# Attention beside a cosine feed-forward: a step's curve, from its sine on, is written behind the next step's attention products

## The chip, the cores and the metric

One core of a Trainium2 chip runs the whole program. The metric is device time of one execution, in microseconds; the profile's span is the time from the first instruction to the last of one profiled execution. TensorE (PE) multiplies, VectorE (DVE), ScalarE (ACT) and GpSimd (POOL) do the elementwise work, and SyncE (SP) issues most DMAs. Each takes its instructions in the order of the program.

## The reference

```python
def _attn_ref(q, k, v):                       # q, k, v: 8 x 8 x 576 x 64
    scores = scale * np.matmul(q, k.transpose(0, 1, 3, 2))
    mask_local = (rel >= 0) & (rel < stride)  # heads 0 to 3; stride 32
    mask_strided = (rel >= 0) & (pos[None, :] % stride == pos[:, None] % stride)  # heads 4 to 7
    scores = np.where(masks[None, :, :, :], scores, -1000000000.0)
    attn = np.exp(scores - np.max(scores, axis=-1, keepdims=True))
    attn = attn / (np.sum(attn, axis=-1, keepdims=True) + 1e-09)
    return np.matmul(attn, v)
...
    x = attn_out.transpose(0, 2, 1, 3).reshape(4608, 512)
    h = x @ w_in                              # 512 x 2048
    g = h * np.cos(h)
    return g @ w_out                          # 2048 x 512
```

## The kernel before

**Tokens and steps.** The 4608 tokens are 12 blocks of 384. A block of the feed-forward takes 16 steps, one for each 128 columns of the hidden layer. Numbers are split into a high and a low part (`g_hi`, `g_lo`), so a product takes three matmuls. The step f of block j, in `hidden`, makes 12 matmuls into one of two PSUM banks, `a` and `b` in turn (line 527), and then the curve h cos h: ScalarE scales h to whole turns (`k`, line 533), VectorE reduces (line 534), ScalarE takes the sine (line 537), VectorE multiplies by h (line 542), which frees the bank, ScalarE casts to `g_hi` (line 547) and GpSimd makes the rest `g_lo` (line 548). `chunk` writes one step: `hidden`, the softmax work of attention units, and `outer` (line 555), 9 matmuls into the accumulators `acc0` to `acc2` for the step three before.

**Attention among the steps.** The attention of batches 0 and 1 and blocks 0 and 1 come first (to 187 us). In blocks 2 to 5 (steps n = 3 to 63, some 188 to 510 us) the attention of the other six batches runs among the steps: 42 units, in each batch strided, strided, local, strided, strided, local, local. The table `bursts` says at which step a unit begins. A **burst** stands ahead of a step's hidden products on TensorE: the products of an earlier unit (line 441 strided, 370 local) and the scores of a new one (lines 405 and 339). There are three banks: scores in `acc0`, transposes and half of the local products in `acc1`, products in `acc2`. Line 431 copies the transposed probabilities out of `acc1`, lines 378 and 379 copy local products out of `acc1` and `acc2`, line 449 strided ones out of `acc2`. The transposes of line 427 follow the step's hidden products.

**Softmax of a unit.** VectorE adds the mask out of the score bank (line 282) and takes maxima (283), GpSimd subtracts them (284), ScalarE takes two silus (293, 296), VectorE joins them (297), ScalarE squares (300), VectorE sums and inverts (302, 305), and GpSimd multiplies (306). A local unit's result is turned by VectorE (351) a good step later; a strided one's is transposed by TensorE (427).

**Other work of a step.** Put behind the step's curve by `behind`: splitting the next block's x (lines 473, 486), sums of weight parts for the later blocks (`combine`: GpSimd 608 and 616, VectorE 613, ScalarE 615), weights on their way out (`put_away`, line 637, on SP's queue), and staging (744, 745). A finished row of attention leaves from ScalarE's queue (line 517).

**What sets the order.** `in_turn` ties TensorE's matmuls together as they are written. On the other engines a scheduler orders the instructions; the order in which they are written is the priority, and `order` adds single ties. One such tie (line 288 and 293) holds a unit's silu behind the copies of the products written last (`self.copied`).

Of the kernel before, what the change touches and what calls it, by code (L numbers as in the profile page):

```python
# [13 lines left out]
F32 = mybir.dt.float32  # L14
# [4 lines left out]
AF = mybir.ActivationFunctionType  # L19
ALU = mybir.AluOpType  # L20
# [33 lines left out]
NFC = DFF // P  # L54

LAG = 3
# [14 lines left out]
LOAD_AT = 6  # L71
# [20 lines left out]
def attention_cos_ffn(ctx, tc, qkl, vl, qkvs, w_in, w_out, eye, eye16, mask_l0, mask_l, mask_s, out):  # L92
# [33 lines left out]
    def order(later, first, reason):  # L126
        tc.add_manual_dep(
            later.ins, first.ins.name,
            mybir.DependencyInfo(mybir.DependencyClass.NoSync, mybir.DependencyReason.DATA), reason=reason,
        )  # L130
# [386 lines left out]
                nc.scalar.dma_start(out=xT[:, c, lo:hi], in_=x[:, lo - at:hi - at])  # L517

    hiddens = itertools.count()

    made_early = {}

    def hidden(j, f, x_hi, x_lo, begun=False):
        h = ps_h.tile([P, 512], F32, name="ab"[next(hiddens) % 2])[:, :TB]
        ops = [(w, x, c) for c in range(NKC) for w, x in ((wi_h, x_hi), (wi_h, x_lo), (wi_l, x_hi))]
        for i, (w, x, c) in enumerate(ops):
            mm = nc.tensor.matmul(h, w[f][:, c], x[c], start=(i == 0), stop=(i == len(ops) - 1))  # L527
            if j >= 2 or begun:
                in_turn(mm)

        r = rp.tile([P, TB], F32, name="r")
        k = r.bitcast(I32)
        nc.scalar.activation(out=k, in_=h, func=AF.Copy, scale=1.0 / (2.0 * math.pi), bias=0.25)
        red = nc.vector.scalar_tensor_tensor(out=r, in0=k, scalar=-2.0 * math.pi, in1=h, op0=ALU.mult, op1=ALU.add)  # L534
        if j < 2:
            reduced[j, f] = red
        sin = nc.scalar.activation(out=r, in_=r, func=AF.Sin, bias=quarter)  # L537
        if j < 2:
            sines[j, f] = sin
        if j == 0 and f == 0:  # L540
            order(sin, exps[-1], "one change of tables")
        chain["curve"] = nc.vector.tensor_tensor(out=r, in0=r, in1=h, op=ALU.mult)  # L542
        if begun:
            g_hi, g_lo = (w[NFC - 1 - f].rearrange("p c n -> p (c n)")[:, :TB] for w in (wi_h, wi_l))
        else:
            g_hi, g_lo = (gp.tile([P, TB], F32R, name=name) for name in ("g_hi", "g_lo"))
        chain["cast"] = nc.scalar.copy(out=g_hi, in_=r)  # L547
        chain["rest"] = nc.gpsimd.tensor_tensor(out=g_lo, in0=r, in1=g_hi.bitcast(F32), op=ALU.subtract)  # L548
        return g_hi, g_lo

    def outer(j, f, g_hi, g_lo, acc, tiles=range(NTT)):
# [25 lines left out]

    pend = []

    def chunk(j, f, x, acc, transposed=(), scored=()):  # L580
        pend.append((j, f, *(made_early.pop((j, f), None) or hidden(j, f, *x)), acc))
        for unit in (*transposed, *scored):
            next(unit)
        if len(pend) > LAG:
            outer(*pend.pop(0))

    def accumulators(pool):
        return [pool.tile([P, DM], F32, name=f"acc{t}") for t in range(NTT)]

    def burst(multiplied, scored):  # L590

        products, tiles = next(multiplied) if multiplied else ((), None)
        scores, others = next(scored) if scored else ((), None)
        if tiles == others:
            matmuls = [m for pair in itertools.zip_longest(products, scores) for m in pair if m]
        else:
            matmuls = [*products, *scores]
        for matmul in matmuls:
            matmul()
        if multiplied:  # L600
            next(multiplied, None)

    def combine(sp, q):

# [156 lines left out]
    with ExitStack() as attending:  # L761
        ps = attending.enter_context(tc.tile_pool(name="ps", bufs=1, space=bass.MemoryType.PSUM, reuse_waits="tile"))
        summing = ExitStack()
        sp = summing.enter_context(tc.tile_pool(name="sp", bufs=1, reuse_waits="tile"))
        att = Attention(attending, False, *(((ps, f"acc{i}"),) for i in range(3)), ld_bufs=2)
        units = [unit for b in range(2, B) for unit in att.units(b)]
        begun = np.interp(range(len(units) + UNIT_LAG), [n for _, n in KNOTS], [at for at, _ in KNOTS])
        bursts = {}
        multiplied = {}
        for kind in (False, True):  # L770
            alike = [k for k in range(len(units)) if bool(STRIDED[k % len(STRIDED)]) == kind]
            multiplied.update(zip(alike[KIND_LAG:], alike))
        left = sorted({*range(len(units))} - {*multiplied.values()})
        multiplied.update(zip(range(len(units), len(units) + UNIT_LAG), left))
        for k, at in enumerate(begun.astype(int).tolist()):
            bursts.setdefault(at, []).append(
                [units[m] if 0 <= m < len(units) else None for m in (k - TURN_LAG, multiplied.get(k, -1), k)]
            )
        putting = put_away()
        sums, last = [], []  # L780
        for q in range(NQ):
            parts = 6 * [combine(sp, q)]
            sums += [last + parts[:1], *([part] for part in parts[1:5])]
            last = parts[5:]
        sums.append(last)
        nxt = direct[3] = x_operands()
        for n in range(LAG, (PLAIN - 2) * NFC):
            j, f = 2 + n // NFC, n % NFC
            if f == 0:
                cur, acc = nxt, accumulators(ps_o)  # L790
            transposed, scored = [], []
            for turned, *units_ in bursts.get(n, ()):
                burst(*units_)
                if turned:
                    transposed.append(turned)
                if units_[1]:
                    scored.append(units_[1])
            if f == LOAD_AT and 2 < j < PLAIN - 1:
                nxt = load_x(j + 1)

            chunk(j, f, cur, acc, transposed, scored)
            if SPLIT_AT <= f < SPLIT_AT + NKC and 2 < j < PLAIN - 1:
                split_loaded(nxt, f - SPLIT_AT)
            next(putting, None)
            if n >= SUMS_AT and sums:
                for part in sums.pop(0):
                    next(part, None)
            if n == STAGED_AT:
                assert not sums
                summing.close()  # L810
                xg = ctx.enter_context(tc.tile_pool(name="xg", bufs=1, reuse_waits="tile"))
                a_pieces = in_pairs(in_xs + in_slots(range(X_AT, X_AT + 6))), in_pairs(
                    in_slots(range(X_AT + 6, X_AT + 20))
                )
                staged = [staging(xg, 0, k, a_pieces[k]) for k in range(2)]
            if n in STAGED:
                next(staged[STAGED[n]])

    rp2, gp2, hp, up, yp = (
        ctx.enter_context(tc.tile_pool(name=name, bufs=bufs, side="right", reuse_waits="tile"))  # L820
# [218 lines left out]
```

## Time and profile before

| | |
|---|---|
| median of 3 runs | 906.04 us (905.9 to 906.94) |
| the profiled execution | 905.24 us, its span 903.2 us |
| TensorE, VectorE, ScalarE, GpSimd busy | 98%, 56%, 58%, 48% of the span |
| granted TensorE clock | 0.998 of full speed |
| HBM read and written | 125.4 MB and 39.6 MB, 183 GB/s over the span |

Engines run side by side, so the shares don't add up. A busy share near 100% says which engine has no time left; what an idle share of another engine is worth has to be read from what it waits for.

### The profile page before, as it was taken

The numbers are of one execution on the slowest core, as the hardware profiler recorded it, in microseconds if no ns is written. First come the engines' busy times: TensorE is split into PE (matmuls) and PEld (weight loads), VectorE is DVE, ScalarE is ACT, GpSimd is POOL, SyncE is SP. The second block draws the span as 40 slices with busy tenths as digits, with TensorE's granted clock in tenths as the row PEclk, the third lists the DMA queues.
The fourth block names the chain that finished last, engine by engine and source line by source line (L and its number), as shares of the span: only waits on it lengthen the run. The fifth ranks groups of instructions, "written<-read, shape, count | busy, mean of one in ns | idle before, by whom it ended". The sixth has DMA issues, their size and how long they took to land.

```text
span 903.2 us, 20455 instructions
## 1 busy us (share of the span) xinstructions
PE 888.3 (98%) x7872; PEld 781.9 (87%) x7872; DVE 501.7 (56%) x966; ACT 522.0 (58%) x1093; POOL 434.8 (48%) x466
## 2 busy tenths in 40 slices
PE   8899999999999999999999999999999999999998
PEld 5689999988888888888888889898998999898997
DVE  5767556455656555556663356555564555554453
ACT  3777777466666656666665455445555545544454
POOL 2766665435756576666744524333343334222231
PEclk9999999999999999999999999999999999999999
DMA  8734334145578867454546756556675656755401
GB/s 292 241 130 142 139 139 161 36 164 175 191 242 278 284 223 239 139 185 139 172 143 217 237 161 221 188 195 209 199 269 173 226 164 197 247 186 187 140 24 70
DMA packets 93408, 166.32 MB, mean 184 GB/s; under 512 B 10752, under 2 KB 34304, under 8 KB 93312
## 3 DMA queue, kind: packets, MB, share of 16 engines
q1 hardware_dynamic: 85248, 157.59, 53.1%
q10 hardware_dynamic: 8064, 7.44, 2.4%
q8 instruction: 62, 1.02, 0.5%
q14 instruction: 34, 0.28, 0.1%
HBM read 125.40 MB, written 39.58 MB: 183 GB/s over the span
## 4 chain that ended last, share of the span: by engine, by line
PE 64%; POOL 4%; ACT 2%; issue 2%; DVE 1%; DMA 0%; SPq 0%; POOLq 0%; ACTq 0%
PE acc L875 22%; PE a L846 11%; PE acc L555 9%; PE b L846 8%; PE b L527 5%; PE a L527 4%; PE acc L370 1%; POOL g_lo L548 1%; POOL t_sb L284 1%; PE acc L441 1%; PE acc L339 1%; PE acc L427 1%; ACT raised L293 1%; DVE r L542 1%; POOL sr L616 0%
## 5 line engine op out<-in xcount | busy, mean ns | idle before, releaser
L861 POOL TENSOR_TENSOR g_lo<-r,g_hi 128x384 fp32r<-128x384 f32 x96 | 98.8, 1030 | 247.7 <-ACT g_hi L860 144.9
L548 POOL TENSOR_TENSOR g_lo<-r,g_hi 128x384 fp32r<-128x384 f32 x94 | 102.4, 1090 | 178.5 <-ACT g_hi L547 101.5
L875 PE MATMUL acc<-s,g_hi 128*128 128x512 f32 x576 | 179.7, 393 | 0.0
L555 PE MATMUL acc<-s,g_hi 128*128 128x512 f32 x564 | 177.6, 396 | 0.0
L555 PEld LDWEIGHTS acc<-s,g_hi 128*128 128x128 f32 x564 | 103.1, 188 | 15.2
L875 PEld LDWEIGHTS acc<-s,g_hi 128*128 128x128 f32 x576 | 106.2, 188 | 10.8
L875 PE MATMUL acc<-s,g_lo 128*128 128x512 f32 x288 | 112.8, 392 | 0.0
L555 PE MATMUL acc<-s,g_lo 128*128 128x512 f32 x282 | 109.8, 390 | 0.0
L527 PE MATMUL a<-x_hi,s 128*128 128x384 f32 x384 | 108.6, 343 | 0.0
L527 PE MATMUL b<-x_hi,s 128*128 128x384 f32 x384 | 108.4, 343 | 0.0
L855 DVE SCALAR_TENSOR_TENSOR r<-r,h 128x384 f32<-128x384 int32 x96 | 58.3, 607 | 88.3 <-ACT r L854 88.3
L846 PE MATMUL a<-s,s 128*128 128x384 f32 x384 | 83.2, 338 | 0.0
L857 DVE TENSOR_TENSOR r<-r,h 128x384 f32<-128x384 f32 x96 | 70.3, 733 | 22.0 <-ACT r L856 20.6
L856 ACT ACTIVATE r<-r,biases 128x384 f32<-128x384 f32 x96 | 59.2, 617 | 36.7 <-DVE r L855 36.6
L860 ACT CAST g_hi<-r 128x384 fp32r<-128x384 f32 x96 | 49.2, 512 | 46.1 <-DVE r L857 45.9
L854 ACT ACTIVATE r<-h 128x384 int32<-128x384 f32 x96 | 50.5, 526 | 40.0 <-DVE h L924 26.0
L846 PEld LDWEIGHTS a<-s,s 128*128 128x128 f32 x384 | 69.4, 188 | 4.2
L537 ACT ACTIVATE r<-r,biases 128x384 f32<-128x384 f32 x96 | 58.6, 611 | 24.5 <-DVE r L534 21.9
L527 PEld LDWEIGHTS b<-x_hi,s 128*128 128x128 f32 x384 | 70.1, 188 | 2.7
L527 PEld LDWEIGHTS a<-x_hi,s 128*128 128x128 f32 x384 | 70.1, 188 | 2.6
L547 ACT CAST g_hi<-r 128x384 fp32r<-128x384 f32 x94 | 48.2, 513 | 35.9 <-DVE r L542 33.5
L527 PE MATMUL a<-x_lo,s 128*128 128x384 f32 x192 | 64.5, 336 | 0.6 <-POOL x_lo L473 0.6
(147 smaller groups left out, 1732.6 us busy)
## 6 DMA issues: line engine op xcount, KB each, us to landing
s<-wis SPq DMA_DIRECT2D x168, 256.0 KB, 3.0
s<-wos SPq DMA_DIRECT2D x96, 256.0 KB, 3.7
qk<-in_qkvs SPq DMA_DIRECT2D x32, 324.0 KB, 3.7
qk<-in_qkl SPq DMA_DIRECT2D x24, 416.0 KB, 4.5
raw<-in_w_in SPq DMA_DIRECT2D x16, 512.0 KB, 4.4
raw<-in_w_out SPq DMA_DIRECT2D x16, 512.0 KB, 3.6
wos<-s SPq DMA_DIRECT2D x32, 256.0 KB, 4.3
wis<-sr SPq DMA_DIRECT2D x32, 256.0 KB, 2.4
```

The lines of the kernel that those rows point to most:

```text
L527: mm = nc.tensor.matmul(h, w[f][:, c], x[c], start=(i == 0), stop=(i == len(ops) - 1))
L537: sin = nc.scalar.activation(out=r, in_=r, func=AF.Sin, bias=quarter)
L548: chain["rest"] = nc.gpsimd.tensor_tensor(out=g_lo, in0=r, in1=g_hi.bitcast(F32), op=ALU.subtract)
L555: mm = nc.tensor.matmul(acc[t], g[:, ts], w[f], start=(f == 0 and i == 0), stop=(f == NFC - 1 and i == 2))
L846: in_turn(nc.tensor.matmul(bank, w[:, n, c], part, start=start and i == 0, stop=stop and i == len(ops) - 1, skip_group_check=True,))
L854: nc.scalar.activation(out=k, in_=h, func=AF.Copy, scale=1.0 / (2.0 * math.pi), bias=0.25)
L855: nc.vector.scalar_tensor_tensor(out=r, in0=k, scalar=-2.0 * math.pi, in1=h, op0=ALU.mult, op1=ALU.add)
L856: nc.scalar.activation(out=r, in_=r, func=AF.Sin, bias=quarter)
L857: chain["curve"] = nc.vector.tensor_tensor(out=r, in0=r, in1=h, op=ALU.mult)
L860: chain["cast"] = nc.scalar.copy(out=g_hi, in_=r)
L861: chain["rest"] = nc.gpsimd.tensor_tensor(out=g_lo, in0=r, in1=g_hi.bitcast(F32), op=ALU.subtract)
L875: in_turn(nc.tensor.matmul(acc, g[gn][:, ts], w[wn], start=done == 0 and i == 0, stop=done == NFC - 1 and i == 2,))
```

## The change

Within blocks 2 to 5, `hidden` no longer writes the second half of its curve (sine, multiplication, cast, rest). It puts these four into `held`, and the loop writes them after the burst of the next step, ahead of that step's own products. The work that stands behind the curve (`work`: splits, weights out, sums; and staging) moves with it. If the burst had local products, the sine is also tied behind the copy of line 379. So a step now writes: burst, the curve of the step before, its work, its own hidden products, k and reduction, softmax, outer products.

```diff
+    held = []
...
-    def hidden(j, f, x_hi, x_lo, begun=False):
+    def hidden(j, f, x_hi, x_lo, begun=False, hold=False):
...
-        sin = nc.scalar.activation(out=r, in_=r, func=AF.Sin, bias=quarter)
...
-        chain["curve"] = nc.vector.tensor_tensor(out=r, in0=r, in1=h, op=ALU.mult)
...
-        chain["cast"] = nc.scalar.copy(out=g_hi, in_=r)
-        chain["rest"] = nc.gpsimd.tensor_tensor(out=g_lo, in0=r, in1=g_hi.bitcast(F32), op=ALU.subtract)
+        def curve(first=None):
+            sin = nc.scalar.activation(out=r, in_=r, func=AF.Sin, bias=quarter)
+            if first is not None:
+                order(sin, first, "copies first")
...
+            chain["curve"] = nc.vector.tensor_tensor(out=r, in0=r, in1=h, op=ALU.mult)
+            chain["cast"] = nc.scalar.copy(out=g_hi, in_=r)
+            chain["rest"] = nc.gpsimd.tensor_tensor(out=g_lo, in0=r, in1=g_hi.bitcast(F32), op=ALU.subtract)
+
+        if hold:
+            held.append(curve)
+        else:
+            curve()
         return g_hi, g_lo
...
         if multiplied:
             next(multiplied, None)
+        return tiles == "32x64"
...
-        for n in range(LAG, (PLAIN - 2) * NFC):
+        def work(n):
             j, f = 2 + n // NFC, n % NFC
-            if f == 0:
-                cur, acc = nxt, accumulators(ps_o)
-            transposed, scored = [], []
-            for turned, *units_ in bursts.get(n, ()):
-                burst(*units_)
...
-            chunk(j, f, cur, acc, transposed, scored)
             if SPLIT_AT <= f < SPLIT_AT + NKC and 2 < j < PLAIN - 1:
                 split_loaded(nxt, f - SPLIT_AT)
             next(putting, None)
             if n >= SUMS_AT and sums:
                 for part in sums.pop(0):
                     next(part, None)
+        def closed():
+            while held:
+                held.pop()(att.copied if local else None)
+
+        for n in range(LAG, steps):
+            j, f = 2 + n // NFC, n % NFC
+            transposed, scored, local = [], [], False
+            for turned, *units_ in bursts.get(n, ()):
+                local = burst(*units_) or local
...
+            closed()
+            if n > LAG:
+                work(n - 1)
...
+            chunk(j, f, cur, acc, transposed, scored, True)
```

TensorE's order is the same in both programs. On ScalarE, at the step whose hidden products begin at 358.38 us (a burst with local products ahead of it), from its k activation to its last cast; before the change (line 537 is the sine, 547 and 615 the casts, 378 and 379 the copies of local products, 293, 296 and 300 the silus and the square):

```order
L533 ACTIVATE r<-b 128x384
L293 ACTIVATE raised_2544<-t_sb,biases 128x6x54
L296 ACTIVATE t_sb<-t_sb,biases 128x324
L537 ACTIVATE r<-r,biases 128x384
L300 ACTIVATE raised_2544<-raised_2544 128x6x54
L547 CAST g_hi<-r 128x384
L615 CAST sr<-sf 128x256
L378 COPY x_l<-acc_5243 128x192
L379 COPY x_l<-acc_5242 128x192
L517 DMA xT<-x_l 128x192 x2
```

and with the change, where the sine is line 544, the casts are lines 552 and 626, and k is line 534:

```order
L534 ACTIVATE r<-b 128x384
L293 ACTIVATE raised_2544<-t_sb,biases 128x6x54
L296 ACTIVATE t_sb<-t_sb,biases 128x324
L300 ACTIVATE raised_2544<-raised_2544 128x6x54
L378 COPY x_l<-acc_5229 128x192
L379 COPY x_l<-acc_5228 128x192
L544 ACTIVATE r<-r,biases 128x384
L517 DMA xT<-x_l 128x192 x2
L552 CAST g_hi<-r 128x384
L626 CAST sr<-sf 128x256
```

The copies moved ahead of the sine, and the square with them; the sine, the DMA issues and both casts follow. Eleven of the 18 local bursts of this part have their sine moved behind softmax work in this way; at the other seven little softmax work stands there, and the copies move ahead of sine and cast alone.

On VectorE, around the multiplication of 271.63 us (line 542; 534 is the reduction, 351 the turn of a local unit, which reads what GpSimd's line 306 writes), before:

```order
L302 TENSOR_REDUCE z<-raised_2543 128x6
L305 RECIPROCAL z<-z 128x6
L534 SCALAR_TENSOR_TENSOR r<-r,b 128x384
L542 TENSOR_TENSOR r<-r,b 128x384
L613 TENSOR_TENSOR sf<-a_3750,sf 128x256
L351 STREAM_TRANSPOSE pt_l<-t_sb 128x384
L282 TENSOR_TENSOR t_sb<-acc_2559,ml 128x384
```

and with the change (multiplication 551, reduction 535):

```order
L302 TENSOR_REDUCE z<-raised_2543 128x6
L305 RECIPROCAL z<-z 128x6
L535 SCALAR_TENSOR_TENSOR r<-r,b 128x384
L351 STREAM_TRANSPOSE pt_l<-t_sb 128x384
L551 TENSOR_TENSOR r<-r,b 128x384
L624 TENSOR_TENSOR sf<-a_3750,sf 128x256
L282 TENSOR_TENSOR t_sb<-acc_2559,ml 128x384
```

The turn moved ahead of the multiplication. The same is so at the copies of 223, 316 and 368 us. On GpSimd, line 306 moved ahead of the rest of the curve at most of the local bursts.

On ScalarE, from the k activation of 419.06 us, before:

```order
L533 ACTIVATE r<-a 128x384
L431 COPY pt<-acc_6231 128x324
L293 ACTIVATE raised_2544<-t_sb,biases 128x6x64
L537 ACTIVATE r<-r,biases 128x384
L296 ACTIVATE t_sb<-t_sb,biases 128x384
L547 CAST g_hi<-r 128x384
L300 ACTIVATE raised_2544<-raised_2544 128x6x64
L449 COPY x_t<-acc_6264 128x6x18x3
```

and with the change:

```order
L534 ACTIVATE r<-a 128x384
L431 COPY pt<-acc_6227 128x324
L544 ACTIVATE r<-r,biases 128x384
L552 CAST g_hi<-r 128x384
L293 ACTIVATE raised_2544<-t_sb,biases 128x6x64
L449 COPY x_t<-acc_6256 128x6x18x3
L296 ACTIVATE t_sb<-t_sb,biases 128x384
L300 ACTIVATE raised_2544<-raised_2544 128x6x64
```

Sine and cast moved ahead of the first silu here. In three other steps (the sines of 320.41, 350.31 and 373.33 us) the sine alone moved ahead of the silus. On SP's queue the weights on their way out (line 637) stand behind the loads that the next burst's units make, by about a step.

## Rows read from the trace of the kernel before

**Rows 1.** The page's head: the span, and each engine's busy us, share of the span and instructions.
```profile
span 903.2 us, 20455 instructions
PE 888.3 (98%) x7872; PEld 781.9 (87%) x7872; DVE 501.7 (56%) x966; ACT 522.0 (58%) x1093; POOL 434.8 (48%) x466
```
**Rows 2.** Busy time by stretch of blocks 2 to 5 (from:to, length, then each engine's busy us and instructions, the granted clock, the share of DMA and its GB/s).
```profile
187.60:350.00 162.40, 162.26 (x2203) 141.46 (x2203) 95.78 (x218) 104.90 (x238) 100.62 (x125) 1.00 0.71 230
350.00:455.00 105.00, 101.76 (x1503) 87.41 (x1504) 63.48 (x141) 66.83 (x156) 66.66 (x82) 1.00 0.51 168
```
**Rows 3.** All waits of TensorE's matmuls from 187.6 to 510 us: who waited for whom, us in total, times, the longest.
```profile
PE acc L427 <- ACT x_l L378: 3.2, 4, 1.1
```
**Rows 4.** TensorE in order of time (start, us, engine, line, tiles, then the idle time before it and what ended it): the start of a step's hidden products (L527) and its transposes (L427), at an undisturbed step and at those that wait; L339 are scores, which follow the local products of L370.
```profile
263.69 0.52 PE L427 MATMUL acc<-ident,pn_s 128*128 128x128 f32 x3
...
271.99 0.45 PE L527 MATMUL a<-x_hi,s 128*128 128x384 f32 x1
...
274.19 0.49 PE L427 MATMUL acc<-ident,pn_s 128*128 128x128 f32 x3
...
357.57 0.87 PE L339 MATMUL acc<-qk 64*32 64x64 f32 x48
358.38 0.44 PE L527 MATMUL a<-x_hi,s 128*128 128x384 f32 x1
...
361.84 0.52 PE L427 MATMUL acc<-ident,pn_s 128*128 128x128 f32 x3 [1.11 <-ACT x_l L378]
...
366.00 0.44 PE L527 MATMUL b<-x_hi,s 128*128 128x384 f32 x1
...
368.92 0.52 PE L427 MATMUL acc<-ident,pn_s 128*128 128x128 f32 x3 [0.57 <-ACT x_l L378]
...
390.77 0.41 PE L427 MATMUL acc<-ident,pn_s 128*128 128x128 f32 x2 [0.78 <-ACT x_l L378]
...
440.32 0.44 PE L427 MATMUL acc<-ident,pn_s 128*128 128x128 f32 x2 [0.78 <-ACT x_l L378]
```
**Rows 5.** ScalarE in order of time from 358.3 to 368.8 us.
```profile
358.36 0.57 ACT L293 ACTIVATE raised<-t_sb,biases 128x324 f32<-128x324 f32 x1 [0.89 <-POOL t_sb L284]
358.97 0.57 ACT L296 ACTIVATE t_sb<-t_sb,biases 128x324 f32<-128x324 f32 x1
359.44 0.60 ACT L537 ACTIVATE r<-r,biases 128x384 f32<-128x384 f32 x1
360.10 0.48 ACT L300 ACTIVATE raised<-raised 128x324 f32<-128x324 f32 x1
360.66 0.51 ACT L547 CAST g_hi<-r 128x384 fp32r<-128x384 f32 x1
...
361.39 0.31 ACT L378 COPY x_l<-acc 128x192 f32<-128x192 f32 x1
...
361.73 0.81 ACTq L517 DMA_DIRECT2D xT<-x_l  x2
...
365.15 0.62 ACT L293 ACTIVATE raised<-t_sb,biases 128x384 f32<-128x384 f32 x1 [1.75 <-POOL t_sb L284]
365.67 0.60 ACT L537 ACTIVATE r<-r,biases 128x384 f32<-128x384 f32 x1
...
368.46 0.32 ACT L378 COPY x_l<-acc 128x192 f32<-128x192 f32 x1
```
**Rows 6.** GpSimd in order of time from 357.5 to 365.2 us.
```profile
357.59 0.74 POOL L284 TENSOR_TENSOR t_sb<-t_sb,mx 128x324 f32<-128x324 f32 x1
361.25 0.99 POOL L548 TENSOR_TENSOR g_lo<-r,g_hi 128x384 fp32r<-128x384 f32 x1 [2.92 <-ACT g_hi L547]
362.21 0.74 POOL L608 TENSOR_TENSOR a<-s,s 128x256 f32<-128x256 f32 x1
...
363.60 0.73 POOL L306 TENSOR_TENSOR pn_s<-raised,z 128x324 f32<-128x324 f32 x1
364.30 0.82 POOL L284 TENSOR_TENSOR t_sb<-t_sb,mx 128x384 f32<-128x384 f32 x1
```
**Rows 7.** VectorE in order of time: the multiplication and the reciprocal of the step at 358.38, and the next step's reduction.
```profile
360.07 0.56 DVE L542 TENSOR_TENSOR r<-r,b 128x384 f32<-128x384 f32 x1
...
361.41 0.19 DVE L305 RECIPROCAL z<-z 128x6 f32<-128x6 f32 x1
...
363.18 0.56 DVE L534 SCALAR_TENSOR_TENSOR r<-r,a 128x384 f32<-128x384 int32 x1 [0.56 <-ACT r L533]
```
**Rows 8.** Four engines in order of time, 271.3 to 276.7 us: the probabilities of a local unit, the multiplication of the step before the transposes, the copy pt, and the products that read it.
```profile
271.36 0.82 POOL L306 TENSOR_TENSOR t_sb<-raised,z 128x384 f32<-128x384 f32 x1
...
271.63 0.55 DVE L542 TENSOR_TENSOR r<-r,b 128x384 f32<-128x384 f32 x1 [0.68 <-ACT r L537]
...
275.17 0.42 ACT L431 COPY pt<-acc 128x324 f32<-128x324 f32 x1
...
276.69 0.26 PE L441 MATMUL acc<-pt,v 54*64 54x54 f32 x1
```
**Rows 9.** ScalarE in order of time at 421.8 us: the sine that follows the first silu.
```profile
421.85 0.60 ACT L537 ACTIVATE r<-r,biases 128x384 f32<-128x384 f32 x1
```
**Rows 10.** ScalarE in order of time at 338.7 us: a copy of local products and the square that follows it.
```profile
338.71 0.29 ACT L378 COPY x_l<-acc 128x192 f32<-128x192 f32 x1
339.81 0.48 ACT L300 ACTIVATE raised<-raised 128x324 f32<-128x324 f32 x1 [0.81 <-DVE raised L297]
```

More of the change, by code (lines that the diff above doesn't have):

```diff
@@ L536, in hidden @@
             reduced[j, f] = red
-        sin = nc.scalar.activation(out=r, in_=r, func=AF.Sin, bias=quarter)
[L538 to L541, printed above, removed]
-        chain["curve"] = nc.vector.tensor_tensor(out=r, in0=r, in1=h, op=ALU.mult)
         if begun:
@@ L546, in hidden @@
             g_hi, g_lo = (gp.tile([P, TB], F32R, name=name) for name in ("g_hi", "g_lo"))
-        chain["cast"] = nc.scalar.copy(out=g_hi, in_=r)
-        chain["rest"] = nc.gpsimd.tensor_tensor(out=g_lo, in0=r, in1=g_hi.bitcast(F32), op=ALU.subtract)
+        def curve(first=None):
+            sin = nc.scalar.activation(out=r, in_=r, func=AF.Sin, bias=quarter)
+            if first is not None:
+                order(sin, first, "copies first")
+            if j < 2:
+                sines[j, f] = sin
+            if j == 0 and f == 0:
+                order(sin, exps[-1], "one change of tables")
+            chain["curve"] = nc.vector.tensor_tensor(out=r, in0=r, in1=h, op=ALU.mult)
[5 more added lines that the diff above has]
+            curve()
         return g_hi, g_lo
@@ L578, in attention_cos_ffn, with chunk @@
     pend = []
-    def chunk(j, f, x, acc, transposed=(), scored=()):
-        pend.append((j, f, *(made_early.pop((j, f), None) or hidden(j, f, *x)), acc))
+    def chunk(j, f, x, acc, transposed=(), scored=(), hold=False):
+        pend.append((j, f, *(made_early.pop((j, f), None) or hidden(j, f, *x, hold=hold)), acc))
         for unit in (*transposed, *scored):
@@ L786, in attention_cos_ffn @@
         nxt = direct[3] = x_operands()
-        for n in range(LAG, (PLAIN - 2) * NFC):
+        def work(n):
             j, f = 2 + n // NFC, n % NFC
-            if f == 0:
-                cur, acc = nxt, accumulators(ps_o)
-            transposed, scored = [], []
-            for turned, *units_ in bursts.get(n, ()):
-                burst(*units_)
[L794 to L799, printed above, removed]
-            chunk(j, f, cur, acc, transposed, scored)
             if SPLIT_AT <= f < SPLIT_AT + NKC and 2 < j < PLAIN - 1:
@@ L807, in attention_cos_ffn @@
                     next(part, None)
-            if n == STAGED_AT:
+        def closed():
+            while held:
+                held.pop()(att.copied if local else None)
+        steps = (PLAIN - 2) * NFC
+        for n in range(LAG, steps):
[3 more added lines that the diff above has]
+                local = burst(*units_) or local
+                if turned:
+                    transposed.append(turned)
+                if units_[1]:
+                    scored.append(units_[1])
+            closed()
+            if n > LAG:
+                work(n - 1)
+            if n - 1 == STAGED_AT:
                 assert not sums
@@ L815, in attention_cos_ffn @@
                 staged = [staging(xg, 0, k, a_pieces[k]) for k in range(2)]
-            if n in STAGED:
-                next(staged[STAGED[n]])
+            if n - 1 in STAGED:
+                next(staged[STAGED[n - 1]])
+            if f == 0:
+                cur, acc = nxt, accumulators(ps_o)
+            if f == LOAD_AT and 2 < j < PLAIN - 1:
+                nxt = load_x(j + 1)
+            chunk(j, f, cur, acc, transposed, scored, True)
+        local = False
+        closed()
+        work(steps - 1)
+        if steps - 1 in STAGED:
+            next(staged[STAGED[steps - 1]])
     rp2, gp2, hp, up, yp = (
```

## The prediction, made before the changed kernel was run

> **What bounds the kernel now.** The page comes first: TensorE is busy 98% of the 903.2 us span [rows 1]. The change touches the steps between 187.6 and about 510 us, so the busy time by stretch comes next: TensorE is idle 0.1 us of 162.4 up to 350 us, and 3.2 us of 105 from there to 455 us [rows 2]. The table of waits puts those 3.2 us on one cause: four times the transposes of line 427 waited for the copy of line 378 [rows 3]. Both use the bank acc1: the copy empties the local products from it, the transposes fill it next. Step by step this is worth a little more, since the pipe also drains: from the start of a step's hidden products to its transposes take 2.20 us undisturbed (271.99 to 274.19), but 3.46 at 358.38 and 2.92 at 366.00; together with 390.77 and 440.32 (0.78 idle each), and a delay of 0.3 at 263.69 that shows no idle time, about 4.2 us hang on this wait [rows 4]. That is all that the change can win.
>
> Why the copy is late is read on ScalarE [rows 5]: at 358.38 its products were done by 357.6, where the scores follow them, and it began at 361.39, behind silu, silu, sine, square, cast and weight cast in ScalarE's order. Why those are late is read on GpSimd [rows 6] and VectorE [rows 7]. There is a **loop from one step's scores to the next's**: subtraction L284 releases silu L293; then come sine L537, multiplication L542 (VectorE), cast L547, GpSimd's g_lo L548, the weight sums L608 and L616, the probabilities L306, and then, because GpSimd takes them in this order, the next L284. From 357.59 to 364.30 each of these starts within about 0.1 us of what releases it. The loop took 6.71 us there, and the TensorE step around it 7.6 with its wait. So ScalarE at 64%, and GpSimd at 63%, of the stretch from 350 to 455 us are not idle capacity: the loop has about the length of a step, and a curve that comes later delays the next step's softmax.
>
> **The change, part by part.** No instruction is added or removed, and TensorE's own order does not change; the counts of busy instructions stay, so all cost or gain is in waits.
>
> *Copies ahead of the sine: the gain.* At 358.38 the new order is silu, silu, square, copies, sine. Silu 358.36 and 358.97 stand as before (no sine came between them); L297 ends 360.06, the square 360.58, and a copy follows 0.1 us before its predecessor's end: 360.5 to 360.8. The transposes start 0.15 us after the copy's end (361.70 to 361.84), so at 360.95 in place of 361.84: **0.9 us won** of 1.26.
>
> *The sine behind the copies: the loss.* The second copy starts 360.75, the sine 360.95 in place of 359.44, and ends 361.55. VectorE has by then done L302 and L305; it multiplies from 361.6 to 362.15. The cast runs 362.2 to 362.7, g_lo starts 362.8 in place of 361.25, that is 1.55 later. L306 now stands ahead of it, in the time that GpSimd waits, which gives 0.70 back. With g_lo's 0.97, L608's 0.70 and L616's 0.69 from start to start, L284 starts at 365.15 in place of 364.30: **0.85 us lost in the loop**, while TensorE has come 0.9 us earlier.
>
> *The next step* shows what that does. There the order is silu, silu, output copy, square, output copy, copies. Silu starts 366.00 in place of 365.15; the second waits for the first to end (0.61 in the step before): 366.6; L297 0.61 later, to 367.8; the square to 368.3, the output copy from 368.25, the copy 368.7 to 369.0. The transposes start at 369.2 in place of 368.92. TensorE had won 0.9 and is now **0.28 behind** where it was before the change: the two waits of 1.26 and 0.72 have become about 0.35 and 1.9.
>
> *The bounds of the excess.* Where the sine stood between the two silus (most strided steps, and 365.67), leaving it out also exposes 0.1 us of the second silu. Where VectorE's new order puts the turn L351 ahead of the multiplication, the multiplication also waits for L306: at 271.36 L306 runs to 272.18, L351 to 272.8, and the multiplication starts about 272.75 in place of 271.63, 1.1 us more [rows 8]. With lateness carried in from the steps before, L351 waits for an L306 that is itself late, so 1.1 is the lower bound for such a place; with no wait for L306 it would be 0, and 2.6 is the largest value that I find when the lateness is carried. At 337.37 the old order had the copy ahead of the square; the new one has it behind, 1 to 1.5 us later (338.71 against the square's end at 340.29) [rows 10].
>
> *What hides the lateness, and when the cover is gone.* The probabilities are used two bursts later, so L284 may slip. At 356.7 to 364.30 it lies 7.6 us behind the scores' burst and TensorE was waiting; in calm stretches 4 to 5.5. About 2 us are therefore free, once. After that late things in turn stop TensorE: pt's copy L431 (275.60, against products at 276.69: 1.1 us of cover [rows 8]), the score bank that L282 empties, the product bank that L449 empties, and the transposes again.
>
> *What gives time back.* In four steps (one at 421.85 [rows 9]) the new order puts the sine ahead of the silus, so the curve does not wait for L284; in one more the multiplication moves ahead of L351. Carried lateness shrinks there by one sine and one multiplication or so, 0.6 + 0.55 = 1.1 us, up to 2.4 where the cast goes ahead too.
>
> *The DMA queues.* SP's order changes: loads of q and k go ahead of the weights' way out by a step. No wait of TensorE in [rows 3] is for a load, so I put this at nothing; its cover is the two buffers of those loads, and without them a load's way would be a few us once. On ScalarE the two issues of L517 now run beside the sine and not just ahead of the next k activation (361.73 to 362.54, the next k activation waiting): up to 0.8 us per local step back for k, but k has to wait for the later cast (362.7) anyway, so I count 0.
>
> *A rule against it.* What waits at the head of ScalarE holds all behind it: at 363.73 the sine's operand was ready, and it ran at 365.67, behind a silu that waited until 365.15 [rows 5, 7]. The Trainium skill has the rule for it ("TensorE: Matmul & The Clock Gate", section on the array of 32x32 parts): ScalarE and VectorE are strict first-in-first-out. By that rule the trade above is forced; if ready work could pass, only the gain would be left, 905.2 - 4.2 = 901.0. The trace agrees with the rule.
>
> *The sum.* I carried the loop's rows through the new order from 219 to 470 us in this way, an estimate by hand. L284's lateness against the old times: +1.4 at the first copies (223), 1.0 of it still there at 254, +1.2 at 263, +1.1 at 272, +0.7 at 289, +0.75 at 310, +2.65 at 316 (turn ahead of the multiplication), +2.5 at 338 (copy behind the square), +0.85 and +0.7 at 361 and 368, +0.9 at 390, +1.4 at 417, +0.5 at 440: 14.65 from 1.4 on. Given back: 0.4 at 247, 1.8 at 321 to 326, 0.9 at 350, 1.1 at 373, 2.4 at 421: 6.6. Left: 8.0 us. TensorE follows the loop about 1 us less late, out of the free 2: **+7 us**. The waits of before that vanish (263, 358, 390, 440) are already in it. The profiled execution took 905.24, 0.8 under the median of 906.04, within what runs differ: 905.24 + 7 = 912.2, I say 912.
>
> **The rivals.** (a) *The lateness is absorbed*, and the gain stays: the carried lateness never passes the free 2 us, because steps without scores let the loop catch up. For it: TensorE idles nowhere between 187.6 and 350 but 0.1 us. Against: in [rows 6] GpSimd waits for the cast, not for TensorE. All of 4.2 or three quarters: 901.0 to 902.1 against the profiled execution's time, 901.8 to 902.9 against the median. Chance 0.22. (b) *Gain and loss cancel*, as at 358 and 366 (0.28 between them), or the copy's release simply moves from the sine to the square, so that the change does not do what it says: 904 to 907. Chance 0.12. (c) *The hidden bank binds*: the multiplication frees the bank that the step after next fills. At 358.38 it would end 362.15 and the bank is wanted only after 372, so it decides only when a curve is over 5 us late; then about 1 us in each of ten late steps, on top: 919. Chance 0.06, within slower. The forecast itself: 0.60.
>
> **How the numbers follow.** About 0.2% (1.8 us) is what a measurement of this kernel can tell from no change. Faster 0.22 (a), same 0.12 (b), slower 0.66 (the forecast, 907.5 to 917, and c). Bounds for the forecast: excess of 0.5 in place of 0.85 to 1.1 per place takes some 4 us off (908); nothing given back adds 6 (918). Forecast and (b) hold 0.72 of the chance, so the range must reach into (a): 901.8 to 918, which leaves out (c) and the tails.
>
> **What would show it.** Right: transposes at the first copies no later than now; from about 275 on new idle rows of TensorE before line 441 or 370 products and before the transposes, ended by ScalarE's copies; L284 behind its scores' burst by 7 us and more in most bursts; the stretch from 187.6 to the end of the attention longer by some 7 us, the stages after 510 us unchanged. Wrong: TensorE without idle rows throughout (then a); idle before L427 unchanged in sum (b); a hidden product waiting for the multiplication (c). The forecast fails if the loop is not the limit that I take it for: if L284 at 274 comes less than 1 us later than now.

## The result, and the profile after

The changed kernel takes 914.78 us (median of 6 runs, 913.73 to 918.72), the kernel before 906.49 in the same comparison (6 runs); the ratio is 1.0097, with a 95% interval of 1.0074 to 1.0119. The change makes the kernel slower by 8.3 us. The prediction was 912.0 us, with 901.8 to 918.0 as its range.

The head of the page, and all waits of TensorE's matmuls from 187.6 to 515 us (who waited for whom, us in total, times, the longest), which answer to [rows 1, 3]:

```profile
span 912.8 us, 20464 instructions
PE 894.2 (98%) x7872; PEld 784.5 (86%) x7872; DVE 504.0 (55%) x966; ACT 521.4 (57%) x1093; POOL 434.4 (48%) x466
```
```profile
PE acc L427 <- ACT x_l L378: 5.1, 5, 1.9
PE acc L441 <- ACT pt L431: 1.6, 3, 1.0
PE acc L441 <- ACT x_t L449: 0.7, 2, 0.6
PE acc L370 <- ACT x_t L455: 0.7, 2, 0.4
PE b L528 <- DVE r L551: 0.3, 1, 0.3
PE acc L565 <- ACT o L585: 0.2, 1, 0.2
```

The one wait of before, transposes for the copy of line 378, has grown from 3.2 to 5.1 us although the copies were moved ahead, and five kinds of wait are new. TensorE in order of time shows where they lie (start, us, engine, line, tiles, and the idle time before with what ended it; hidden products are line 528 now):

```profile
265.61 0.52 PE L427 MATMUL acc<-ident,pn_s 128*128 128x128 f32 x3 [0.78 <-ACT x_l L378]
...
301.96 0.44 PE L528 MATMUL b<-x_hi,s 128*128 128x384 f32 x1 [0.35 <-DVE r L551]
307.73 0.32 PE L441 MATMUL acc<-pt,v 54*64 54x54 f32 x2 [0.99 <-ACT pt L431]
...
348.26 0.52 PE L427 MATMUL acc<-ident,pn_s 128*128 128x128 f32 x3 [1.94 <-ACT x_l L378]
...
378.83 0.52 PE L427 MATMUL acc<-ident,pn_s 128*128 128x128 f32 x3 [1.49 <-ACT x_l L378]
```

Three of the waits of [rows 4] are gone: those of 361.84, 390.77 and 440.32. The wait of 368.92 has become 1.49 (378.83 here), the small delay of 263.69 a wait of 0.78 (265.61), and the transposes at 348.26, which waited for nothing before, wait 1.94.

TensorE's order is the same in both, so its intervals can be compared one by one, from each change of the kind of product to the next, 187.7 to 512 us:

| interval | us won | us lost |
|---|---|---|
| hidden products to transposes | 2.9 | 5.2 |
| outer products to the next burst | 0.0 | 3.9 |
| burst to its hidden products | 0.0 | 1.2 |
| hidden to outer products | 0.1 | 1.0 |
| others | 0.1 | 0.2 |

Together +8.3 us, the difference of the medians. (The profiled execution's span is longer by 9.6; 1.2 of that is there before the first burst and so is not the change's. In that part the granted clock was 0.50, the lower of its two levels, 1.2 GHz, from 35.9 to 42.7 us, after 10.1 us of which TensorE was busy 8.25; the kernel before shows 1.00 there.) From the hidden products of 512.07 us (521.57 after) to TensorE's last matmul the two take 387.4 and 387.5 us.

**One pair of steps, row by row.** These are the two steps of [rows 5, 6], which now begin at 368.08 and 374.98. TensorE, ScalarE (sine 544, cast 552) and GpSimd (g_lo 553; the sums 619 and 627 stand between it and L284) in order of time:

```profile
368.08 0.45 PE L528 MATMUL a<-x_hi,s 128*128 128x384 f32 x1
...
370.57 0.52 PE L427 MATMUL acc<-ident,pn_s 128*128 128x128 f32 x3
...
374.98 0.44 PE L528 MATMUL b<-x_hi,s 128*128 128x384 f32 x1
```
```profile
368.01 0.57 ACT L293 ACTIVATE raised<-t_sb,biases 128x324 f32<-128x324 f32 x1 [0.79 <-POOL t_sb L284]
369.74 0.48 ACT L300 ACTIVATE raised<-raised 128x324 f32<-128x324 f32 x1 [0.56 <-DVE raised L297]
370.12 0.30 ACT L378 COPY x_l<-acc 128x192 f32<-128x192 f32 x1
370.53 0.62 ACT L544 ACTIVATE r<-r,biases 128x384 f32<-128x384 f32 x1
371.78 0.51 ACT L552 CAST g_hi<-r 128x384 fp32r<-128x384 f32 x1 [0.62 <-DVE r L551]
...
378.36 0.32 ACT L378 COPY x_l<-acc 128x192 f32<-128x192 f32 x1
```
```profile
367.25 0.72 POOL L284 TENSOR_TENSOR t_sb<-t_sb,mx 128x324 f32<-128x324 f32 x1
371.12 0.74 POOL L306 TENSOR_TENSOR pn_s<-raised,z 128x324 f32<-128x324 f32 x1 [3.14 <-PE acc L427]
372.37 1.01 POOL L553 TENSOR_TENSOR g_lo<-r,g_hi 128x384 fp32r<-128x384 f32 x1 [0.52 <-ACT g_hi L552]
...
374.71 0.83 POOL L284 TENSOR_TENSOR t_sb<-t_sb,mx 128x384 f32<-128x384 f32 x1
```

The copy comes 2.1 us after the silu (3.0 before), so the transposes at 370.57 start 2.49 after their step's hidden products (3.46 before): 0.97 won. The sine comes 2.5 us after the silu (1.1 before), g_lo 4.4 (2.9 before), and the next L284 comes 7.46 us after the last (6.71 before). The next copy stands behind that L284's silus, and its transposes start 3.84 after their hidden products (2.92 before): 0.92 lost. With 0.25 lost between the two, ahead of the second step's hidden products, the pair ends 0.2 us worse than before the change.

**A place where the turn got ahead.** ScalarE, GpSimd and VectorE at the copies that stood at 316 us before:

```profile
323.82 0.63 ACT L544 ACTIVATE r<-r,biases 128x384 f32<-128x384 f32 x1
...
320.22 0.83 POOL L284 TENSOR_TENSOR t_sb<-t_sb,mx 128x384 f32<-128x384 f32 x1
...
324.46 0.83 POOL L306 TENSOR_TENSOR t_sb<-raised,z 128x384 f32<-128x384 f32 x1 [3.41 <-ACT r L544]
326.96 1.01 POOL L553 TENSOR_TENSOR g_lo<-r,g_hi 128x384 fp32r<-128x384 f32 x1 [1.67 <-ACT g_hi L552]
...
329.34 0.83 POOL L284 TENSOR_TENSOR t_sb<-t_sb,mx 128x384 f32<-128x384 f32 x1
...
325.32 0.58 DVE L351 STREAM_TRANSPOSE pt_l<-t_sb 128x384 f32<-128x384 f32 x1 [1.00 <-POOL t_sb L306]
325.83 0.51 DVE L551 TENSOR_TENSOR r<-r,b 128x384 f32<-128x384 f32 x1
```

The same two L284 before the change:

```profile
312.66 0.82 POOL L284 TENSOR_TENSOR t_sb<-t_sb,mx 128x384 f32<-128x384 f32 x1
...
319.02 0.83 POOL L284 TENSOR_TENSOR t_sb<-t_sb,mx 128x384 f32<-128x384 f32 x1
```

The sine ends at 324.45, but VectorE holds the multiplication behind the turn, which waits for GpSimd until 325.3: the multiplication starts at 325.83, 1.4 us after its operand. From one L284 to the next it is 9.12 us here and 6.36 before: 2.76 us lost in one loop.

### The profile page after: what moved, and what is told of

The parts are those of the page before. It is cut to its first block, busy times and chain, and to the rows that moved or that the text cites. A ratio compares the mean times of both kernels' runs of the same rounds, so it can differ in the third digit from the quotient of the medians.

```text
span 912.8 us, 20464 instructions
## 1 busy us (share of the span) xinstructions
PE 894.2 (98%) x7872; PEld 784.5 (86%) x7872; DVE 504.0 (55%) x966; ACT 521.4 (57%) x1093; POOL 434.4 (48%) x466
## 4 chain that ended last, share of the span: by engine, by line
PE 51%; POOL 8%; ACT 5%; issue 4%; DVE 3%; DMA 2%; SPq 0%; ACTq 0%; POOLq 0%
PE acc L902 22%; PE a L873 11%; PE b L873 8%; PE acc L565 4%; PE a L528 2%; PE b L528 2%; POOL t_sb L284 2%; POOL g_lo L553 2%; POOL sr L627 1%; POOL a L619 1%; DMA wis<-s 1%; DVE r L551 1%; ACT raised L293 1%; ACT r L544 1%; DVE raised L297 1%
```

## The experiments

The theory: the sine behind the copies lengthens the loop from one L284 to the next, and the loop is what a late curve delays; TensorE loses time only when the loop's lateness reaches it. Rivals: SP's new order (the weights' way out behind the loads); a cost of copies or sine that TensorE pays directly; sheer work on GpSimd. Each kernel was timed against the kernel before on the same chip. The stretch is TensorE's, from the end of the first unit's scores to the end of the last unit's (190.66 to 465.84 before); L284's **lag** is counted from the end of its own unit's scores, the mean of 42. Its **lateness**, used below, is something else: how much later it starts than in the kernel before, both counted from the end of the first unit's scores.

| kernel | ratio to before (95%) | stretch, us | mean lag of L284, us |
|---|---|---|---|
| before | | 275.2 | 4.2 |
| the change | 1.0097 (1.0074 to 1.0119) | 283.5 | 5.7 |
| e1, order of SP alone | 1.0003 (0.9988 to 1.0017) | 275.6 | 4.3 |
| e2, tie alone | 1.0098 (1.0081 to 1.0116) | 284.2 | 5.8 |
| e3, turn behind the multiplication | 1.0064 (1.0044 to 1.0085) | 280.1 | 5.5 |
| e4, cast tied | 1.0075 (1.0056 to 1.0094) | 283.5 | 5.3 |
| e5, before without sums | 0.9967 (0.9954 to 0.9981) | 270.6 | 2.6 |
| e6, change without sums | 0.9965 (0.9950 to 0.9979) | 272.8 | 4.0 |
| e7, four steps | 1.0014 (0.9999 to 1.0029) | 276.7 | 4.5 |
| e8, copies into idle time | 0.9957 (0.9943 to 0.9971) | 272.3 | 3.9 |
| e9, change, sums behind L284 | 0.9969 (0.9954 to 0.9983) | 272.5 | 3.9 |

The ratios are of medians, stretch and lag of one profiled execution each. In e4's profiled execution the granted clock was 0.50, the lower level, from 309.7 to 313.1 us, just after TensorE had waited 1.7 us for `pt`, and one step took 1.5 us longer in it. Without that its stretch would be some 282. Whether the wait brought the clock down no run shows.

**e1 and e2: which half of the change.** e1 keeps the held curve and drops the tie; e2 keeps the tie and issues the weights' way out (`putting`) at its old place, behind `chunk`.

```diff
e1, in closed():
-                held.pop()(att.copied if local else None)
+                held.pop()(None)
e2, in work(n), and behind chunk(...):
-            next(putting, None)
...
+            next(putting, None)
```

> The curve is still held and written behind the next burst, but the sine is not tied behind the copies. The order on VectorE, GpSimd and TensorE is then that of before, on ScalarE too but for one pair of casts; what stays of the change is SP's order, where the weights on their way out stand behind the next burst's loads. Theory (the tie alone costs, the queue's order nothing): 906.5, within 1.8 us of before, and no TensorE waits beyond the four of before. Rival (the later weights' way out, or the loads they cross, is what TensorE loses): 913 to 915, as the whole change.

> The complement: sine tied behind the copies as in the change, but the weights on their way out issued at their old place, so that SP's order is nearly that of before while ScalarE, VectorE and GpSimd have exactly the order of the change. Theory: 914.8, within 1.8 us of the change, L284 late by 7 us and more from 350 us on. Rival (the queue's order): 905 to 908.

907.60 and 915.43 us against 906.86 before. Writing the curve a step later moves next to nothing on the elementwise engines (VectorE's and GpSimd's orders are those of before, ScalarE's but for one cast), and neither that nor the queue's order costs anything that the interval shows; e1's TensorE has the four waits of before and one of 0.45 us at the copies of 263. The tie behind the copies is the whole loss.

**e3: the turn.** The turn of a local unit is tied behind the multiplication.

```diff
-                nc.vector.transpose(out=pt[:, :LU * KW], in_=pn.rearrange("p t w -> p (t w)"))
+                turned = nc.vector.transpose(out=pt[:, :LU * KW], in_=pn.rearrange("p t w -> p (t w)"))
+                if not self.plain:
+                    behind(turned, "curve")
```

> The change, with the turn of a local unit (L351) tied behind the multiplication of the curve, so that it no longer stands ahead of it at the copies of 223, 272, 316 and 368 us. My sum put 1.1 us and more on each of these places (lateness of L284 +1.4, +1.1, +2.65 and +0.85 there). Theory (these are terms of the loop): the lateness of L284 is 4 to 5 us smaller by 375 us, and the time 909 to 911.5. Rival (the turn is not on the loop's path; the sine behind the copies costs all of it): 913.5 to 916, as the change. Second rival (the later turn makes products that read it late): above 916.

912.35 us. The stretch is 3.4 us shorter than the change's, and L284's lateness at the loop after 368 us is 6.7 in place of 10.0 us: 3.3 less, under the 4 to 5 expected, and the time lies just above what I gave. The tie does more than I meant: 16 of the 17 turns of this part stand behind a later multiplication than in the change, not only the four that had got ahead of theirs. At those four places L284 loses 3.8 us less than in the change; elsewhere it loses 0.5 more. The other 5 to 6 us of the loss stay, so the turn is a part and not the whole.

**e4: the cast in place of the sine.**

```diff
+        sin = nc.scalar.activation(out=r, in_=r, func=AF.Sin, bias=quarter)
+        chain["curve"] = nc.vector.tensor_tensor(out=r, in0=r, in1=h, op=ALU.mult)
...
         def curve(first=None):
...
             chain["cast"] = nc.scalar.copy(out=g_hi, in_=r)
+            if first is not None:
+                order(chain["cast"], first, "copies first")
```

> Sine and multiplication are written and run at their old place; only the cast, the rest and the step's other work are written behind the next burst, and the cast instead of the sine is tied behind the copies. Copies pass the cast and the weight cast only. From the rows at 358 us: the copy starts at 360.66 in place of 361.39 (0.7 won), the cast at 361.3 in place of 360.66, the rest of the curve 0.65 later, and L306 runs in the gap, so L284 is late by 0 to 0.4. Theory (loss = what the tie adds to the loop from scores to scores): 903 to 906.5, L284 late by under 2 us at 350 us. Rival (anything of the curve behind the copies costs the same, since the rest of the curve ends later all the same): 910 to 915.

913.19 us: my expectation failed, and its rival was right. I had costed it at 358 us alone, where the square ends before the cast. ScalarE at the copies of 223 us shows what I missed, before the change and then in e4:

```profile
220.48 0.62 ACT L293 ACTIVATE raised<-t_sb,biases 128x384 f32<-128x384 f32 x1 [0.36 <-POOL t_sb L284]
...
222.23 0.51 ACT L547 CAST g_hi<-r 128x384 fp32r<-128x384 f32 x1
```
```profile
222.29 0.62 ACT L293 ACTIVATE raised<-t_sb,biases 128x384 f32<-128x384 f32 x1 [0.52 <-POOL t_sb L284]
...
224.55 0.52 ACT L300 ACTIVATE raised<-raised 128x384 f32<-128x384 f32 x1 [0.63 <-DVE raised L297]
224.98 0.30 ACT L378 COPY x_l<-acc 128x192 f32<-128x192 f32 x1
225.18 0.32 ACT L379 COPY x_l<-acc 128x192 f32<-128x192 f32 x1
225.39 0.52 ACT L551 CAST g_hi<-r 128x384 fp32r<-128x384 f32 x1
```

The copies stand behind the square, the square waits for VectorE, and before the change the cast ran in that wait: 1.75 us after the silu (222.23 against 220.48), now 3.1 (225.39 against 222.29). What is tied behind the copies is tied behind the softmax ahead of them too; L284 loses 1.3 us there.

**e5 and e6: the loop without the sums.** L608 and L616 (619 and 627 with the change) are left out of both kernels, and what goes out in their place goes in two transfers of half the size.

```diff
-            t = sp.tile([P, 2 * P], F32, name=f"a{n}{k}")
...
-            behind(nc.gpsimd.tensor_tensor(out=t, in0=w[0], in1=w[1], op=ALU.add), "rest")
-            return t
+            return w[0]
...
-            nc.gpsimd.tensor_tensor(out=part[:, 1], in0=t, in1=part[:, 0].bitcast(F32), op=ALU.subtract)
-            nc.sync.dma_start(out=wis[q][i], in_=part.bitcast(F32))
+            for n in range(2):
+                nc.sync.dma_start(out=wis[q][i][:, n], in_=part[:, 0].bitcast(F32))
```

> The kernel before without GpSimd's weight sums (L608 and L616, 0.73 us each, one or two in a step from 223 to 446 us): the first summand is used as the sum, and the low parts are not formed, so the blocks after 510 us multiply by other weights; the same instructions and transfers run there. Theory (a loop from one step's scores to the next's, with these two in it): the loop is 0.7 to 1.4 us shorter, the four waits of TensorE for the copies shrink, 902 to 905. Rival (the copies are late for ScalarE's own order, whatever GpSimd does): 905 to 907.

> The change without the same weight sums (the first summand is used as the sum, the low parts are not formed). Theory (the loop's length is what turns a later sine into lost time): L284's lateness no longer adds up from burst to burst, and the time is 0 to 3 us above that of the kernel before without sums, in place of 8. Rival (the copies and the sine cost TensorE directly, with the sums or without): 7 to 9 us above it.

903.36 and 903.38 us, against 907.04 before. Without the sums the kernel before has none of its four waits left and gains 3.0 us by the ratio; the change on top of it costs nothing that the medians show, each good to some 1.3 us (2.2 us by the stretches of the two profiled executions, 1.5 of it one wait of the transposes), where with the sums it costs 8.3. The sine is tied behind the copies there as in the change. So the tie costs TensorE little or nothing directly: the length of the loop that it is put into does.

**e7: the tie at four bursts alone.** `hold` is true only ahead of the steps at 358.38, 366.00, 387.64 and 437.18.

```diff
+COPIES_FIRST = {34: None, 35: None, 39: None, 48: None}
...
-            chunk(j, f, cur, acc, transposed, scored, True)
+            chunk(j, f, cur, acc, transposed, scored, n + 1 in COPIES_FIRST)
```

> The change at four of the 18 local bursts alone, those of the four waits (hidden products from 358.38, 366.00, 387.64 and 437.18 us); at all others the curve is written and run as before. Theory: 0.9, 0.8 and 0.8 won at three of them, at 366.00 nothing, since two output copies still stand ahead of the copies; 0.85 lost in the loop at each, which calm steps around 390 and 440 take up: 904 to 906.5. If the loss were a matter of every burst alike, four of 18 would cost 1.8 us: 907 to 909.

907.62 us against 907.04, 1.3 us slower by the ratio, with no change just inside the interval; I had expected a small gain. A cost at every burst alike would have given this time too, but the rows show 0.8 us more of L284's lateness at 358, 366 and 390 and none at 437. TensorE in order of time (transposes are line 430 there, the copy 381):

```profile
372.34 0.52 PE L430 MATMUL acc<-ident,pn_s 128*128 128x128 f32 x3 [1.47 <-ACT x_l L381]
...
416.54 0.52 PE L430 MATMUL acc<-ident,pn_s 128*128 128x128 f32 x3 [0.71 <-ACT x_l L381]
...
461.82 0.52 PE L430 MATMUL acc<-ident,pn_s 128*128 128x128 f32 x3 [0.82 <-ACT x_l L381]
```

The waits of 390 and 440 are gone and that of 358 is 0.17, but the one of 368.92 has become 1.47 (372.34), and transposes that waited for nothing before, in steps that the edit leaves alone, now wait 0.71 and 0.82. L284's lateness stays at 1.5 to 1.6 us from 393 to 470 us: calm steps don't take it up, and the local bursts among them show it.

**e8: the copies where ScalarE idles.** At the same four bursts the silu of the unit whose softmax was written last (at the fourth the square) is tied behind the copies as well.

```diff
+COPIES_FIRST = {34: 0, 35: 0, 39: 0, 48: 1}
...
+                self.softened.append((silu, square))
...
                 local = burst(*units_) or local
+                if COPIES_FIRST.get(n) is not None:
+                    order(att.softened[-1][COPIES_FIRST[n]], att.copied, "copies first")
```

> At the same four bursts the copies are moved further, into the time in which ScalarE waits for GpSimd's L284 (0.89 idle ahead of the silu of 358.36, 0.79 ahead of that of 387.29): the silu there, and at 437 the square, is tied behind the copies, and the sine too. Two copies take 0.5 us, so silu and sine start hardly later than before. Theory (a copy costs nothing where ScalarE waits, and delays the loop where it stands ahead of ready work): most of the 3.5 us of these four waits is won, 902.5 to 904.5, and L284 is not later than before. Rival (silus that wait for TensorE's products delay the loop as the sine did): 906 to 910.

902.78 us against 907.04, ratio 0.9957: faster than both kernels. ScalarE and TensorE at the first of the four (copies 381 and 382, silu 295, sine 547, transposes 430; hidden products begin at 360.62):

```profile
360.62 0.44 PE L531 MATMUL a<-x_hi,s 128*128 128x384 f32 x1
...
359.95 0.32 ACT L381 COPY x_l<-acc 128x192 f32<-128x192 f32 x1 [0.24 <-PE acc L373]
360.16 0.33 ACT L382 COPY x_l<-acc 128x192 f32<-128x192 f32 x1
360.61 0.57 ACT L295 ACTIVATE raised<-t_sb,biases 128x324 f32<-128x324 f32 x1
361.08 0.60 ACT L547 ACTIVATE r<-r,biases 128x384 f32<-128x384 f32 x1
...
362.81 0.49 PE L430 MATMUL acc<-ident,pn_s 128*128 128x128 f32 x3
```

The copies run right behind their products, in the time that [rows 5] show as 0.89 idle; the silu starts when L284 has ended (360.58), and the transposes 2.19 after their hidden products. The four waits of before are all gone; one of 0.5 us is new, at transposes (456.43) that waited for nothing before. Part of the gain is not the copies': in the new order GpSimd takes L284 ahead of L306 at three of the places, and L284 comes up to 4.8 us earlier there.

**e9: the sums behind L284.** All work of the change, with the sums written a step later and tied.

```diff
-                nc.gpsimd.tensor_tensor(
+                self.lowered = nc.gpsimd.tensor_tensor(
...
+            order(add, att.lowered, "the next softmax first")
...
+            order(low, att.lowered, "the next softmax first")
...
+            if n > LAG:
+                summed_up(n - 1)
```

> The change with all its work, but GpSimd's weight sums written a step later and tied behind the next unit's subtraction L284, so that g_lo is followed by L284 and not by one or two sums of 0.73 us. Theory (what counts is the length of the loop, not the work that GpSimd does): L284 comes 0.7 to 1.4 us earlier after each late curve, its lateness stays under 4 us, and the change loses at most 3 us: 904 to 909. Rival (the runs without sums were fast because there was less work on GpSimd and beside it): 912 to 916, as the change.

903.98 us against 907.11, ratio 0.9969. GpSimd at the place of 316 us, and all that is left of TensorE's waits:

```profile
321.48 1.06 POOL L553 TENSOR_TENSOR g_lo<-r,g_hi 128x384 fp32r<-128x384 f32 x1 [1.67 <-ACT g_hi L552]
322.50 0.82 POOL L284 TENSOR_TENSOR t_sb<-t_sb,mx 128x384 f32<-128x384 f32 x1
323.29 0.73 POOL L619 TENSOR_TENSOR a<-s,s 128x256 f32<-128x256 f32 x1
```
```profile
PE acc L427 <- ACT x_l L378: 0.5, 1, 0.5
PE acc L441 <- ACT pt L431: 0.4, 1, 0.4
```

The curve is as late as in the change (g_lo waits 1.67 for the cast in both), but L284 follows g_lo at once, and the lateness of L284 there is 0.9 us in place of 9.2. The same instructions, 11 us less than the change. The rival of GpSimd's load falls; what counts is what stands between g_lo and L284. No run has the sums behind L284 without the tie, so whether the tie wins or costs anything there is open; e5 and e6 suggest that it does neither.

## Why the prediction was right, and where its steps were off

**The loop** is the mechanism that I named, and it held at most places where I had carried it by hand. What L284's lateness gains or loses from one unit to the next, us, at the places of the sum:

| place | forecast | measured |
|---|---|---|
| 223, 263, 272 | +1.4, +1.2, +1.1 | +1.5, +1.4, +1.1 |
| 247 | -0.4 | -0.1 |
| 289 | +0.7 | +2.0 |
| 310, 316 | +0.75, +2.65 | +0.75, +2.75 |
| 321 to 326 | -1.8 | -1.8 |
| 338, 350 | +2.5, -0.9 | +2.0, -0.8 |
| 361, 368, 373 | +0.85, +0.7, -1.1 | +0.75, +0.75, -1.4 |
| 390, 417, 421 | +0.9, +1.4, -2.4 | +0.8, +1.2, -2.75 |
| 440 | +0.5 | -0.45 |
| not in the sum: 387, 413, 434, 459, 471 | | +0.35, +0.35, +1.05, +0.7, -1.45 |
| smaller steps | | -0.3 |
| in all | +8.0 | +8.4 |

The total agrees better than its parts: 289 is 1.3 short, 440 has the wrong sign, and five steps that the sum lacks add up to 1.0. They nearly cancel, which is luck. That the loop is the limit was an argument from rows; e5, e6 and e9 show it.

**The gain** of copies ahead of the sine is as worked out: 0.9 forecast and 0.97 measured at 358, 2.9 us in sum of the 4.2 that were there. The delay at 263, which the sum lets vanish too, grew from 0.3 to 0.9.

**The step that was off** is the last of the sum: "TensorE follows the loop about 1 us less late, out of the free 2". TensorE ends 8.3 us late and the last L284 8.4, so +7 should have been +8. The cover is not a fixed 2 us. Against the lateness of TensorE at the end of the same unit's scores, L284's is larger by 5.6 us at 316 (9.2 and 3.6), by 0.3 at 358 and by 2.4 at 420 (11.3 and 8.9); TensorE has lost 8.7 us by 372 and is never more than 9.0 late. That the two end together is partly chance, as the last L284 shows, before and after:

```profile
470.64 0.84 POOL L284 TENSOR_TENSOR t_sb<-t_sb,mx 128x384 f32<-128x384 f32 x1
```
```profile
480.19 1.01 POOL L284 TENSOR_TENSOR t_sb<-t_sb,mx 128x384 f32<-128x384 f32 x1 [1.02 <-DVE mx L283]
```

Before the change it stands right behind GpSimd's work for staging (line 745, 469.67 to 470.69); after it, GpSimd is idle and waits for VectorE's maxima of this unit's scores, and 1.4 us of lateness are gone. What sets the cover at each place no run shows. Of the 2.8 us between 912.0 and 914.78, this term is 1.3; 1.25 more is the base, for the sum starts from the profiled execution's 905.24, and the kernel before took 906.49 beside the change.

**What I expected to see.** Unchanged stages after 510 us, new idle time ahead of L441, L370 and the transposes: so it is, and L284 at 274, on which the forecast was to stand or fall, comes 3.9 us later. Transposes no later at the first copies holds for 223; those of 265.6 already wait 0.78. "L284 behind its scores' burst by 7 us and more in most bursts" is wrong: counted from the burst's start, as there, it is so in 19 of 42 (5 before), and the mean lag behind the scores' end grew from 4.2 to 5.7; the scores themselves slip with TensorE, so the lag stays bounded while the lateness adds up.

**The rivals.** (a) and (b) are out by the time; (b)'s second mechanism, a copy that now waits for the square, is there (370.12 above, and e4), but gain and loss don't cancel over the 18 bursts. (c), the hidden bank, does bind, once, for 0.35 us at 301.96, much earlier than the 372 that I named; it costs little. SP's queue was rightly put at nothing (e1). That ready work waits behind what stands ahead of it on its engine is seen again in the multiplication at 325.83 above, held 1.4 us behind a turn that was not ready.

## What to carry to other kernels

An engine that is busy two thirds of the time can still be the limit, if a chain through several of them closes on itself and is as long as a step: follow who releases whom from one softmax to the next, and add up that chain before moving anything in it. An instruction that is tied behind a copy is behind everything that the copy stands behind, so move the copy into an idle gap (e8) rather than ready work behind the copy. And take out of the chain what does not belong to it: sums that can wait, put behind the instruction that closes the loop, turned a loss of 8 us into a gain of 3 (e9).
